# Windowed attention and a dense softplus block on one core: softmax two heads ahead instead of four, sink sums two steps later, exact loads without zeros, and new lists of the order

## The chip, the core and the metric

One core of a Trainium2 chip runs the kernel. The metric is device time in microseconds (us), the median of several executions. The trace comes from one profiled execution. Engines are named PE (TensorE), PEld (its weight loads), DVE (VectorE), ACT (ScalarE), POOL (GpSimd) and SP (SyncE, which issues nearly all DMAs).

## The reference

```python
# q, k, v: 4 x 8 heads x 768 x 64, float32; n_sink 4, window 128
scores = (q @ k.T) / 8
keep = (key < n_sink) | (0 <= query - key < window)
a = softmax(where(keep, scores, -1e9))
x = (a @ v), heads side by side          # 3072 x 512
h = x @ w_in                             # 512 x 2048, float64 weights
g = max(h, 0) + log1p(exp(-abs(h)))
out = g @ w_out                          # 2048 x 512, float64 weights
```

## The kernel before, in words

The 3072 rows are worked in 12 chunks of 256 (three to a batch of 768), each with 8 heads. A head of a chunk is one step of the attention, and one slice of 256 of the 2048 inner columns is one step of the dense part, whose slices run one chunk (8 steps) behind the attention. A loop over steps i calls the parts of several heads and slices, each at its own distance from i. Each part is a letter:

- L loads a head's keys and queries, p splits them into a rounded high part and a rest (ACT casts, DVE subtracts twice in `split_low`, called at h), S makes the scores on PE, T masks them and takes the row's largest (DVE), e exponentiates (ACT), N or M (two heads at once) inverts the sums (DVE), n scales (POOL or ACT).
- W transposes the weights on PE, t copies them out of PSUM (ACT or DVE), u takes the rest (DVE), B selects the window with four selects on POOL, V multiplies by the values on PE, O adds the halves up (ACT copy, two DVE adds).
- k and K make the four heads' weights on the sink keys: a product on DVE, a transpose on PE, ACT copies, and at y two DVE subtractions and a POOL copy. For an even head V also makes the sink part of a pair of heads with one matmul (line 422), which ACT copies to xs. Z adds it to the pair's sum, X rounds that to xh, x takes the rest xl.
- U is the up projection of a slice (24 matmuls of 256 columns, lines 564 to 582; H is its first half), F the three activations of the softplus (ACT), P the gate (DVE; it frees the PSUM bank of U, of which there are two), g rounds to gh, R takes the rest gl, D and E are the halves of the down projection (6 matmuls of 512 columns each), Y stores.
- G and q load and split values, J and j the sinks' values.

Chunks 0 and 1 are "exact": their heads aren't split, queries of two heads lie beside zeros in one tile (`q0`), so that each head's 64 rows meet keys of 128 partitions, and values likewise (`v0`, line 237), so that each head's matmul writes 128 partitions, half of them zeros.

The weights come in float64, 32 blocks of 512 KB, in the order in which the dense part wants them (wi00, wi01, wi10, wi11, wo00 and so on). Each goes through w (the DMA), a (the top words, line 502), c (the 32-bit word, DVE, line 516), d (the high part) and l (the low part). `WT`, `WH` and `WL` name the engine of a, d and l for each block (A, V for DVE, P for POOL), `WM` whether the word lies in SBUF (s) or PSUM (p; then l is DVE's); `NM`, `TH` and `GH` name those of n, t and g.

All engines run in order. Their orders are set by two lists written by hand or found by a search: `START` (lines 1021 to 1032) for the first 17 steps, where a token such as D1 calls one part at once and z11 issues 11 matmuls that only keep PE busy; then `STEADY` (lines 1011 to 1020), one string for each step modulo 8. A load waits for the buffer that it reuses: tiles "qk" (a split head, or queries of an exact pair) have two.

What sets the distances is this, in `_fast`:

```python
"S": (call(att, "scores"), G),          # G = 4: step i makes head i + 4
"p": (call(att, "split"), G + 1),
"W": (call(att, "weights_t"), c.LEAD),  # LEAD = 0
"k": (call(att, "sink_weights", G), 0),
"L": (call(att, "load"), G + 2),
```

Of the kernel before, what the change touches and what calls it, by code (L numbers as in the profile page):

```python
# [142 lines left out]
class _Attention:  # L143


    def __init__(self, c, chunk):
# [258 lines left out]
    def values(self, h):  # L405
# [19 lines left out]
        for n in range(self.vlo, 3):
# [5 lines left out]
            nc.tensor.matmul(x[:, :, o], w, pt[:, :, m], start=first, stop=last, skip_group_check=True)  # L431
        self.x[h] = x

    def out(self, h):
# [16 lines left out]
        if h % 2 == 1:  # L451
            xf, xs, hi, lo = self.xf, self.xsb, xh[:, h // 2], xl[:, h // 2]
            eng = "V" if h == H - 1 else c.E["xl"]

            def high():
                _copy(nc, c.E["xh"], hi, xf[:])
                c.do("x", lambda: _sub(nc, eng, lo, xf[:], hi))

            def total():
                (nc.vector if h == H - 1 else nc.gpsimd).tensor_tensor(xf[:], xf[:], xs[:], ALU.add)  # L460
                c.do("X", high)

            c.do("Z", total)

    def xs(self, h, t):
        c, nc, chunk = self.c, self.c.nc, self.chunk
        self.xsb = c.sp.tile([P, CT], F32, tag="xs", name=f"xs{chunk}_{h}s", bufs=1)
        _copy(nc, "A", self.xsb[:], t)
# [624 lines left out]
```

## Time and profile before

| | |
|---|---|
| median of 3 runs | 707.87 us (706.4 to 710.44) |
| profiled execution | 706.73 us, span 705.0 us, clock 0.998 |
| PE, PEld busy | 685.4 us (97%), 618.8 us (88%) |
| DVE, ACT, POOL busy | 578.5, 468.0, 377.3 us |
| HBM read, written | 57.40 MB, 6.29 MB |

The span runs from the first to the last instruction. Busy time of an engine counts its instructions' own time, and a row's idle time before them, with the instruction that ended it, tells what the engine waited for. A matmul's end is modelled, so successive matmuls overlap in the rows: the distance of their starts is their pace. PE's granted clock is full throughout the span.

### The profile page before, as it was taken

How to read it: one execution, taken by the hardware profiler on the slowest of the kernel's cores; microseconds unless marked ns; L12 is line 12 of the kernel's file. 1: busy time of each engine (PE TensorE's matmuls, PEld its weight loads, DVE VectorE, ACT ScalarE, POOL GpSimd, SP SyncE). 2: the span in 40 equal slices, each digit the busy share in tenths (PEclk: the TensorE clock that was granted, in tenths of full speed). 3: DMA queues.
4: the chain of work that ended last, by engine and by line, in shares of the span. 5: the costliest groups of instructions: out<-in, count | busy, mean ns of one | idle time of the engine just before them, and what ended most of it. 6: DMA issues, size and time to landing. Idle time of an engine off the chain costs nothing.

```text
span 705.0 us, 13763 instructions
## 1 busy us (share of the span) xinstructions
PE 685.4 (97%) x4454; PEld 618.8 (88%) x4454; DVE 578.5 (82%) x1679; ACT 468.0 (66%) x1176; POOL 377.3 (54%) x716
## 2 busy tenths in 40 slices
PE   7889899999999999999999999999999999999996
PEld 6778788899989999899999989999998989989995
DVE  6999888897898898897898898888898989865452
ACT  5889866667677666767676676767666676754331
POOL 5757465664465664664465565675555556452000
PEclk9999999999999999999999999999999999999999
DMA  8896623123122213221322321312212312100000
GB/s 312 290 384 225 198 73 103 51 73 95 47 81 81 68 52 87 78 66 54 95 69 62 99 70 54 111 47 66 85 51 77 95 46 80 62 13 1 31 2 34
DMA packets 39526, 64.67 MB, mean 92 GB/s; under 512 B 4502, under 2 KB 19990, under 8 KB 39446
## 3 DMA queue, kind: packets, MB, share of 16 engines
q1 hardware_dynamic: 39156, 63.19, 28.4%
q8 instruction: 37, 0.61, 0.4%
q10 hardware_dynamic: 290, 0.52, 0.2%
q14 instruction: 43, 0.35, 0.1%
HBM read 57.40 MB, written 6.29 MB: 90 GB/s over the span
## 4 chain that ended last, share of the span: by engine, by line
PE 85%; DMA 4%; DVE 4%; ACT 3%; POOL 1%; SPq 1%; issue 1%; POOLq 0%; DVEq 0%; ACTq 0%
PE h L575 36%; PE acc L637 12%; PE acc L639 12%; PE acc L638 12%; PE x L431 5%; PE s L278 3%; PE s L277 3%; PE t L371 2%; DMA wo21r<-w 1%; DMA wi71r<-w 1%; PE t L422 1%; DMA wi00r<-w 1%; DVE wt L516 1%; SPq L481 1%; ACT a L306 1%
## 5 line engine op out<-in xcount | busy, mean ns | idle before, releaser
L575 PE MATMUL h<-xh,wi 128*128 128x256 f32 x1536 | 251.9, 286 | 0.0
L575 PEld LDWEIGHTS h<-xh,wi 128*128 128x128 f32 x1536 | 211.4, 191 | 1.3 <-DVE mt L596 0.2
L637 PE MATMUL acc<-wo,gh 128*128 128x512 f32 x384 | 153.2, 399 | 2.2 <-ACT gh L57 2.2
L575 PE MATMUL h<-xl,wi 128*128 128x256 f32 x768 | 154.7, 283 | 0.0
L638 PE MATMUL acc<-wo,gh 128*128 128x512 f32 x384 | 150.8, 393 | 0.0
L639 PE MATMUL acc<-wo,gl 128*128 128x512 f32 x384 | 150.4, 392 | 0.3 <-DVE gl L65 0.3
L588 ACT ACTIVATE mt<-h 128x512 f32<-128x512 f32 x96 | 57.5, 599 | 125.9 <-PE h L575 125.6
L596 DVE SCALAR_TENSOR_TENSOR mt<-h,mt 128x512 f32<-128x512 f32 x96 | 66.0, 688 | 72.7 <-ACT mt L590 56.7
L575 PEld LDWEIGHTS h<-xl,wi 128*128 128x128 f32 x768 | 119.5, 192 | 0.1
L333 POOL TENSOR_SCALAR a<-a,rc 128x128 f32<-128x128 f32 x178 | 82.8, 477 | 34.8 <-DVE rc L319 33.8
L639 PEld LDWEIGHTS acc<-wo,gl 128*128 128x128 f32 x384 | 72.1, 188 | 17.0 <-DVE gl L65 0.7
L637 PEld LDWEIGHTS acc<-wo,gh 128*128 128x128 f32 x384 | 72.3, 188 | 14.7 <-ACT gh L57 2.6
L306 ACT ACTIVATE a<-a,stats 128x136 f32<-128x136 f32 x192 | 76.0, 397 | 13.1 <-DVE stats L297 12.9
L397 POOL TENSOR_SCALAR_AFFINE_SELECT pt<-th 128x256 fp32r<-128x256 f32 (+1 forms) x96 | 46.7, 486 | 66.2 <-ACT th L57 65.9
L638 PEld LDWEIGHTS acc<-wo,gh 128*128 128x128 f32 x384 | 72.4, 189 | 9.9
L397 POOL TENSOR_SCALAR_AFFINE_SELECT pt<-tl 128x256 fp32r<-128x256 f32 x80 | 43.8, 547 | 45.5 <-DVE tl L65 44.1
L65 DVE TENSOR_TENSOR gl<-mt,gh 128x512 fp32r<-128x512 f32 x96 | 67.6, 704 | 0.4 <-DVE gh L59 0.2
L589 ACT ACTIVATE mt<-mt 128x512 f32<-128x512 f32 x96 | 60.8, 634 | 3.1
L590 ACT ACTIVATE mt<-mt 128x512 f32<-128x512 f32 x96 | 60.7, 633 | 3.0
L57 ACT CAST qkh<-qk 128x656 fp32r<-128x656 f32 x80 | 59.0, 739 | 2.6 <-DVE wo L59 1.9
L65 POOL TENSOR_TENSOR vv<-vr,vv 128x384 fp32r<-128x384 f32 (+1 forms) x40 | 37.7, 942 | 29.1 <-ACT vv L57 28.6
L65 DVE TENSOR_TENSOR kl<-qk,qkh 128x400 fp32r<-128x400 f32 x80 | 50.9, 636 | 2.5
(198 smaller groups left out, 1249.8 us busy)
## 6 DMA issues: line engine op xcount, KB each, us to landing
qk<-qk SPq DMA_DIRECT2D x160, 164.0 KB, 2.9
out<-o SPq DMA_DIRECT2D x23, 256.0 KB, 2.1
vr<-v SPq DMA_DIRECT2D x28, 192.0 KB, 2.5
q<-q SPq DMA_DIRECT2D x7, 256.0 KB, 3.3
k<-k SPq DMA_DIRECT2D x8, 200.0 KB, 5.5
vz<-v SPq DMA_DIRECT2D x4, 384.0 KB, 8.2
vr<-v SPq DMA_DIRECT2D x12, 128.0 KB, 2.2
vz<-v SPq DMA_DIRECT2D x4, 256.0 KB, 5.8
```

The costliest lines, as they stand in the source:

```text
L57: nc.scalar.copy(out, in_)
L65: (nc.vector if eng == "V" else nc.gpsimd).tensor_tensor(out, a, b, ALU.subtract)
L306: nc.scalar.activation(a, a, AF.Exp, bias=c.stats[:, k : k + 1], scale=-1.0, accum_out=sm)
L333: (nc.vector if eng == "V" else nc.gpsimd).tensor_scalar(a, a, rc[:, j : j + 1], 0.0, ALU.mult, ALU.add)
L397: nc.gpsimd.affine_select(pt[:, e, :, 1], src[:], [[0, CH], [1, P]], ALU.is_ge, 0.0, base=0, channel_multiplier=-1)
L575: nc.tensor.matmul(h[:, j], wt, x, start=first, stop=last, skip_group_check=True)
L589: nc.scalar.activation(t[:], t[:], AF.Exp, scale=-1.0)
L590: nc.scalar.activation(t[:], t[:], AF.Ln, bias=1.0)
L596: nc.vector.scalar_tensor_tensor(t[:], h[:], 0.0, t[:], ALU.max, ALU.add)
L637: nc.tensor.matmul(acc[:], gh[:, j, q], wh, start=f == 0, stop=False, skip_group_check=True)
L638: nc.tensor.matmul(acc[:], gh[:, j, q], wl, start=False, stop=False, skip_group_check=True)
L639: nc.tensor.matmul(acc[:], gl[:, j, q], wh, start=False, stop=f == 2 * FP - 1, skip_group_check=True)
```

## The change

`AHEAD = 2` takes the place of `G` in the distances of S, T, N, M, p and L; k and K are called two steps later in the loop. The sink part of a pair leaves V and becomes a part of its own, C (`sink_sum`), called at steps 2 and 3 modulo 4. The first chunk's queries are loaded without zeros (each head's matmul then uses 64 rows of the array), the values of both exact chunks too (each head's matmul then has 64 columns). Engines of some steps, `START` and `STEADY` are new. Before, START made the scores of heads 0 to 20, now of 0 to 18.

```diff
+AHEAD = 2
@@ load
-                q = qp.tile([P, 2, CT], F32, tag=qt, name=f"q{chunk}_{h}", bufs=bufs)
-                (nc.scalar if chunk == h == 0 else nc.sync).dma_start(q[:], c.a["q0"][chunk, h // 2])
-                self.heads[h], self.heads[h + 1] = (q[:, 0], k), (q[:, 1], k)
+                if chunk == 0:
+                    q = qp.tile([P, CT], F32, tag=qt, name=f"q{chunk}_{h}", bufs=bufs)
+                    (nc.sync if h else nc.scalar).dma_start(q[:], c.a["q0"][h // 2])
+                    self.heads[h], self.heads[h + 1] = (q[:D], k[:D]), (q[D:], k[D:])
+                else:
+                    q = qp.tile([P, 2, CT], F32, tag=qt, name=f"q{chunk}_{h}", bufs=bufs)
+                    nc.sync.dma_start(q[:], c.a["q1"][h // 2])
+                    self.heads[h], self.heads[h + 1] = (q[:, 0], k), (q[:, 1], k)
@@ load_v
-            vz = pool.tile([P, 3 - lo, 2, P], F32, tag=tag, name=f"vz{chunk}_{g}", bufs=2)
+            vz = pool.tile([P, 3 - lo, 2, D], F32, tag=tag, name=f"vz{chunk}_{g}", bufs=2)
@@ values
-            if not odd:
-                sv = c.vs[self.b, h // G][:, h % G : h % G + 2].rearrange("p h d -> p (h d)")
-                t = _half_bank(c)
-                nc.tensor.matmul(t, sv, self.sk[h // G], start=True, stop=True)
-                self.xs(h, t)
-            nc.tensor.matmul(x[:, :, o], w, pt[:, :, m], start=first, stop=last, skip_group_check=True)
+            r = slice(h % 2 * D, h % 2 * D + D) if self.exact else slice(0, P)
+            nc.tensor.matmul(x[r, :, o], w, pt[:, :, m], start=first, stop=last, skip_group_check=True)
@@ out: the pair's total moves into sink_sum
+    def sink_sum(self, pair):
+        c, nc, chunk, g = self.c, self.c.nc, self.chunk, 2 * pair // G
+        sv = c.vs[self.b, g][:, 2 * pair % G : 2 * pair % G + 2].rearrange("p h d -> p (h d)")
+        t = _half_bank(c)
+        nc.tensor.matmul(t, sv, self.sk[g], start=True, stop=True)
+        xs = c.sp.tile([P, CT], F32, tag="xs", name=f"xs{chunk}_{pair}", bufs=1)
+        _copy(nc, "A", xs[:], t)
+        c.do("Z", lambda: self.total(pair, xs))
...
@@ _fast
+    def sums(i):
+        e = (i - AHEAD) % G
+        if e < 2:
+            call(att, "sink_sum", 2)(i - 2 + e)
-        "S": (call(att, "scores"), G),
+        "S": (call(att, "scores"), AHEAD),
-        "p": (call(att, "split"), G + 1),
+        "p": (call(att, "split"), AHEAD + 1),
-        "k": (call(att, "sink_weights", G), 0),
-        "K": (call(att, "sink", G), 0),
+        "k": (call(att, "sink_weights", G), AHEAD - G),
+        "K": (call(att, "sink", G), AHEAD - G),
+        "C": (sums, 0),
-        "L": (call(att, "load"), G + 2),
+        "L": (call(att, "load"), AHEAD + 2),
...
@@ engines
-Ctx.NM = "APPAAAPPPAPPAAPPP"
-Ctx.TH = "AAAAAAAAAAAVAAAAVA"
-Ctx.GH = "AAPAAAVVV"
-Ctx.WM = "spspsssppssspsssssssssssssssssss"
-Ctx.WT = "PAAVAVAAAAAPAAAVAVAAAAAAAAAPAAVP"
-Ctx.WH = "VPAAPVVAVAVAPAAAAAPAAAAAAAAAAAVV"
-Ctx.WL = "VPPVPVPPVPPVVPPPVVVPVPPVVVVVPVPV"
+Ctx.NM = "APPAAAPPPAPAAAPPP"
+Ctx.TH = "AAAAAAAAAAAVAAAVVA"
+Ctx.GH = "AAAAAPVVV"
+Ctx.WM = "spspsspppssppsssssssssssssssssss"
+Ctx.WT = "PAAVAVAAAAAPAAAVAVAAAAAAAAAVAAVV"
+Ctx.WH = "VPAAPVVAAAVAPAAAAAPAAAAAAAAAAAVV"
+Ctx.WL = "VVPVPVPPPVPVPPVPVVPPVPVVVVVVPVPV"
@@ STEADY
-    "kSWtpDuKYRQThqByUeFPXEngVZxON",
-    "SUpqWktYRZQDKuFTBXehEPNyngVxO",
-    "kpWYtuUByhqFQSDnTKePVZNROgXxE",
-    "WkZpSYUqQTtyhuFPRgDBEenXKVNOx",
-    "kpWYtUquKBSFRyZnQDVThePXNgOxE",
-    "kWUYtRuSTqDBQFepyZPEXNngVhKOx",
-    "knpWtuqUQKhYSTRDFeBZPVgyENOXx",
-    "kWpURYtSuDyqhBFTQPVOZeEgNXKnx",
+    "DWUptqSCQYyEFuhTkRePBNVgKXOZxn",
+    "QpSWYqUDtTFhEekuRNPBgVCyOnXZKx",
+    "pWYtQUkhKFySuqTPnDRxBeCEVXNZgO",
+    "YWQSqUtpDkuFhCTEePgBKNRxynVOXZy",
+    "WptQkUYuyKhXFqPnCSDTREBVxeNgZO",
+    "SWtquUDQEpFTeRkhYPBnyVgOZCNKxX",
+    "WpnUtkKhxyQSFuqDYCETPReBVNZOXg",
+    "YWSqUQtupBkFDChEVTyReOPNZKgXxn",
@@ START
-w J0 z1 S0 S1 T0 T1 w j4 w S2 S3 M0 w T2 S4 a w w T3 W1 c z3 a M2 S5 L8 T4 W0 z11 w S6 S7 T5 a w k0 d K0 c d
...
-l d U2 c F1 a T13 d V9 c D0 a L16 M12 c P1 d l l O8 l c R1 w W10 w O9 w a S14 w d D1 E0 d c U3 d l w a F2 c
-G12 d l l a a T14 L17 l W11 c P2 a c E1 N14 R2 V10 d c w l p16 S15 a F3 w O10 d G14 a d c L18 V11 d U4 P3
-T15 l l E2 l a c c w R3 a a d H5 W12 N15 D2 S16 k12 w O11 c D3 p17 d l F4 K12 a w U5 d G16 W13 l d a T16 l
-V12 P4 l w c L20 W14 S17 U6 c l F5 V13 a T17 E3 d P5 O12 c a U7 L19 R4 p18 E4 p20 J16 c S18 l l D4 F6 R5 l
-N16 D5 O13 p19 T18 W15 E5 S19 N17 G18 T19 L21 V14 q16 P6 F7 N18 c N19 S20 d V15 O14 d T20 L22 R6 W16 k16 O15
-U8 P7 K16 D6 R7 E6 F8 N20 V16 p21 O16 d P8
+w S0 z3 J0 S1 z3 S2 z3 T0 j4 T1 M0 T2 S3 w a z3 w w L8 T3 W1 S4 c a M2 S5 T4 w c k0 w W0 a S6 d z3 z3 S7 T5
...
+w a d H0 M10 k8 w V7 c c O7 d a S12 d l c U0 L16 F0 K8 U1 w a l a c w a d T12 P0 l L14 V8 c w d l d c a R0 w
+l W9 c S13 l a d F1 T13 d w U2 O8 a P1 c V9 D0 M12 a c d H3 l l R1 l c O9 W10 a S14 c d d l w a d F2 U3 l w
+a l c E0 D1 a w d l T14 G12 c P2 W11 c a w c V10 d l S15 p16 R2 a L17 F3 d w O10 c E1 d U4 P3 T15 d a l V11
+a w l G14 W12 D2 w R3 l S16 N14 w c N15 O11 c H5 D3 G16 a E2 c d L18 k12 p17 a F4 d K12 U5 l a w d W13 P4 d
+l V12 O12 c a T16 w W14 l a c E3 d F5 l S17 l T17 P5 R4 U6 a V13 c M16 U7 E4 p18 L20 O13 S18 L19 l c D4 l l
+J16 R5 V14 W15 F6 T18 P6 R6 O14 q16 D5 p19 E5 c V15 H8 O15 W16 F7 N18 U8 d G18 F8 P7 P8 D6 R7 d E6 d V16 O16
```

## Rows read from the trace of the kernel before

**Rows 1.** The page: busy time of PE over the span, and from the table of groups the largest one (busy us, mean ns of one, idle time before).

```profile
PE 685.4 (97%) x4454; PEld 618.8 (88%) x4454; DVE 578.5 (82%) x1679; ACT 468.0 (66%) x1176; POOL 377.3 (54%) x716
L575 PE MATMUL h<-xh,wi 128*128 128x256 f32 x1536 | 251.9, 286 | 0.0
```

**Rows 2.** Busy time by window, one steady chunk: window, its length, then busy us (instructions) of PE, PEld, DVE, ACT and POOL, PE's clock, the DMA engines' share and GB/s.

```profile
267.40:322.70 55.30, 55.30 (x368) 50.30 (x367) 47.91 (x140) 38.16 (x98) 33.43 (x64) 1.00 0.24 72
```

**Rows 3.** The same view, two windows of the start.

```profile
10.00:20.00 10.00, 7.88 (x49) 6.39 (x48) 8.31 (x39) 8.76 (x34) 4.51 (x10) 1.00 1.01 391
50.00:60.00 10.00, 7.54 (x45) 6.07 (x44) 9.54 (x21) 9.78 (x23) 6.46 (x6) 1.00 0.97 322
```

**Rows 4.** PE's waits from 0 to 110 us: who waited for whom, us in total, times, longest.

```profile
PE t L371 <- ACT sk L57: 4.1, 3, 2.4
...
PE s L277 <- DVE qkh L65: 1.2, 1, 1.2
```

**Rows 5.** The chain of work that ended last, from 57 to 112 us: start, us, what. Two of its pieces, an up projection and one matmul of a down projection.

```profile
107.60 2.87 PE h L575 x24
...
110.68 0.23 PE acc L637
```

**Rows 6.** DMA issues of the page: number, KB of one, us from issue to landing. The queries of exact chunks (an eighth is issued by ACT), and the values of chunk 1.

```profile
q<-q SPq DMA_DIRECT2D x7, 256.0 KB, 3.3
...
vz<-v SPq DMA_DIRECT2D x4, 384.0 KB, 8.2
```

**Rows 7.** POOL in order of time at the start: start, us, line, operation, output from input; in brackets the idle time before it and what ended it.

```profile
12.41 0.77 POOL L61 TENSOR_SCALAR upper<-wi00r 128x512 f16<-128x512 bf16 x1 [1.02 <-DMA wi00r<-w]
...
33.19 1.71 POOL L65 TENSOR_TENSOR wi<-wt,wi 128x512 fp32r<-128x512 f32 x1
...
73.43 0.79 POOL L61 TENSOR_SCALAR upper<-wi71r 128x512 f16<-128x512 bf16 x1 [4.01 <-DMA wi71r<-w]
```

**Rows 8.** DVE in order of time, same columns: the word of wi00, a word beside POOL's subtraction, gate P1, the end of the split of head 16, the split of head 21.

```profile
13.22 0.93 DVE L516 SCALAR_TENSOR_TENSOR wt<-wi00r,upper 128x512 int32<-128x512 int32 x1 [1.47 <-POOL upper L61]
...
33.69 1.77 DVE L516 SCALAR_TENSOR_TENSOR word_ps<-wi21r,upper 128x512 int32<-128x512 int32 x1
...
52.38 0.68 DVE L596 SCALAR_TENSOR_TENSOR mt<-h,mt 128x512 f32<-128x512 f32 x1
...
65.84 0.58 DVE L65 TENSOR_TENSOR kl<-qk,qkh 128x400 fp32r<-128x400 f32 x1
...
105.89 0.42 DVE L65 TENSOR_TENSOR qkh<-qk,qkh 64x256 fp32r<-64x256 f32 x1 [1.34 <-ACT qkh L57]
```

**Rows 9.** PE in order of time, same columns: scores S14; the first matmul of D1; transposes of sink weights (K12, 32 columns) and the up projection that follows; transposes W13; transposes W14 and the scores that follow.

```profile
50.55 1.06 PE L274 MATMUL s<-k,q 128*128 128x264 f32 x4
53.77 0.50 PE L637 MATMUL acc<-wo,gh 128*128 128x512 f32 x1 [2.17 <-ACT gh L57]
...
73.95 0.38 PE L352 MATMUL t<-ident,sa 128*32 128x128 f32 x2
74.08 0.72 PE L575 MATMUL h<-xh,wi 128*128 128x256 f32 x4
...
78.17 0.44 PE L371 MATMUL t<-ident,a 128*128 128x128 f32 x2 [2.41 <-ACT sk L57]
...
79.76 0.38 PE L371 MATMUL t<-ident,a 128*128 128x128 f32 x2
79.89 0.37 PE L277 MATMUL s<-qkh 128*128 128x264 f32 x1
```

**Rows 10.** ACT in order of time, same columns: the scalings of M12, gh of P1, the copy of the sink weights of K12.

```profile
51.92 1.28 ACT L331 ACTIVATE a<-a,rc 128x128 f32<-128x128 f32 x4 [0.15 <-DVE rc L319]
53.11 0.61 ACT L57 CAST gh<-mt 128x512 fp32r<-128x512 f32 x1
...
77.75 0.36 ACT L57 COPY sk<-t 32x256 f32<-32x256 f32 x1 [2.29 <-POOL sk L354]
```

**Rows 11.** SP's issues in order of time: the loads of heads 17 and 18.

```profile
64.08 1.20 SPq L214 DMA_DIRECT2D qk<-qk  x2
...
66.97 1.46 SPq L214 DMA_DIRECT2D qk<-qk  x2
```

**Rows 12.** All engines in order of time in a steady chunk, where K, S, D and the sink sum stand behind each other: K, POOL's copy at y, the last matmul of D, the sink sum.

```profile
295.63 0.27 PE L358 MATMUL t<-ident,sa 128*64 128x128 f32 x1
...
297.26 0.40 POOL L61 TENSOR_SCALAR sk<-sk 64x256 fp32r<-64x256 f32 x1 [0.82 <-ACT mt L588]
...
297.36 0.40 PE L639 MATMUL acc<-wo,gl 128*128 128x512 f32 x1
...
297.72 0.39 PE L422 MATMUL t<-sk,vs 128*128 128x256 f32 x1
```

**Rows 13.** The same view at the seam of two chunks: the values of head 7, and of the last pair xh, one step of the normalise and xl.

```profile
318.47 0.62 PE L431 MATMUL x<-pt,vv 128*128 128x256 f32 x3
...
320.89 0.41 ACT L57 CAST xh<-xf 128x256 fp32r<-128x256 f32 x1 [0.48 <-DVE xf L460]
321.11 0.16 DVE L318 TENSOR_SCALAR sm<-sm 128x2 f32<-128x2 f32 x1
321.31 0.17 DVE L319 RECIPROCAL rc<-sm 128x2 f32<-128x2 f32 x1
321.39 0.41 DVE L65 TENSOR_TENSOR xl<-xf,xh 128x256 fp32r<-128x256 f32 x1
```

More of the change, by code (lines that the diff above doesn't have):

```diff
@@ L151, in __init__ @@
         self.exact = chunk < c.EXACT
-        self.heads, self.v, self.a, self.rc, self.sk, self.pt, self.s, self.sm, self.x = {}, {}, {}, {}, {}, {}, {}, {}, {}
+        self.heads, self.v, self.a, self.rc, self.sk, self.pt, self.s, self.sm, self.x, self.xf = {}, {}, {}, {}, {}, {}, {}, {}, {}, {}
     def load_sinks(self):
@@ L445, in out @@
         if h % 2 == 0:
-            self.xf = c.sp.tile([P, CT], F32, tag="xf", name=f"xf{chunk}_{h}")
-        mine = self.xf[r0 : r0 + D]
+            self.xf[h // 2] = c.sp.tile([P, CT], F32, tag="xf", name=f"xf{chunk}_{h}")
+        mine = self.xf[h // 2][r0 : r0 + D]
         _copy(nc, "A", mine, x[D:, 0])
@@ L450, in out, with total, high @@
         nc.vector.tensor_tensor(mine, x[:D, 1], mine, ALU.add)
[L451 to L468, printed above, removed]
+    def sink_sum(self, pair):
[6 more added lines that the diff above has]
+        c.do("Z", lambda: self.total(pair, xs))
+    def total(self, pair, xs):
+        c, nc, xf = self.c, self.c.nc, self.xf.pop(pair)
+        xh, xl = c.x[self.chunk]
+        last = 2 * pair + 2 == H
+        (nc.vector if last else nc.gpsimd).tensor_tensor(xf[:], xf[:], xs[:], ALU.add)
+        def high():
+            _copy(nc, c.E["xh"], xh[:, pair], xf[:])
+            c.do("x", lambda: _sub(nc, "V" if last else c.E["xl"], xl[:, pair], xf[:], xh[:, pair]))
+        c.do("X", high)
 def _weight_dma(c, s, k, half):
@@ L746, in _fast @@
     parts = {
-        "S": (call(att, "scores"), G),
-        "T": (call(att, "softmax"), G),
-        "N": (call(att, "normalise"), G),
-        "M": (call(att, "normalise_two"), G),
-        "p": (call(att, "split"), G + 1),
+        "S": (call(att, "scores"), AHEAD),
+        "T": (call(att, "softmax"), AHEAD),
+        "N": (call(att, "normalise"), AHEAD),
+        "M": (call(att, "normalise_two"), AHEAD),
+        "p": (call(att, "split"), AHEAD + 1),
         "q": (call(att, "split_v", 2), 1),
         "W": (call(att, "weights_t"), c.LEAD),
-        "k": (call(att, "sink_weights", G), 0),
-        "K": (call(att, "sink", G), 0),
+        "k": (call(att, "sink_weights", G), AHEAD - G),
+        "K": (call(att, "sink", G), AHEAD - G),
+        "C": (sums, 0),
         "V": (call(att, "values"), 0),
@@ L1020 @@
 ]
 Ctx.START = """
-w J0 z1 S0 S1 T0 T1 w j4 w S2 S3 M0 w T2 S4 a w w T3 W1 c z3 a M2 S5 L8 T4 W0 z11 w S6 S7 T5 a w k0 d K0 c d
-N4 T6 l c G4 W2 a l L10 V0 V1 d O0 c l N6 G6 O1 W3 a w T7 d c V2 a O2 S8 a N5 N7 W4 V3 T8 L12 c S9 k4 O3 w w
-a z4 K4 c G8 G10 d T9 l W5 d w N9 S10 V4 l a W6 V5 T10 N8 d O4 O5 S11 W7 T11 w l c l z2 V6 V7 w O6 W8 w w a
-c M10 O7 c k8 d w l L14 a d d U0 F0 K8 w S12 l a U1 T12 V8 l c w a c d a P0 S13 c w l d w c d R0 a z2 l a W9
-l d U2 c F1 a T13 d V9 c D0 a L16 M12 c P1 d l l O8 l c R1 w W10 w O9 w a S14 w d D1 E0 d c U3 d l w a F2 c
@@ new lines @@
+K0 T6 d G4 w a W2 c c V0 l d V1 l l N6 O0 O1 a d W3 T7 c L10 w a a V2 z3 M4 S8 z3 w N7 G8 W4 L12 k4 V3 T8 c
+S9 c O2 O3 a G6 K4 w T9 d w G10 W5 d S10 a l l N9 W6 V4 T10 O4 w w N8 V5 d O5 w W7 l S11 T11 V6 W8 c w l O6
+w a d H0 M10 k8 w V7 c c O7 d a S12 d l c U0 L16 F0 K8 U1 w a l a c w a d T12 P0 l L14 V8 c w d l d c a R0 w
+l W9 c S13 l a d F1 T13 d w U2 O8 a P1 c V9 D0 M12 a c d H3 l l R1 l c O9 W10 a S14 c d d l w a d F2 U3 l w
+a l c E0 D1 a w d l T14 G12 c P2 W11 c a w c V10 d l S15 p16 R2 a L17 F3 d w O10 c E1 d U4 P3 T15 d a l V11
@@ L1061, in _layout @@
     k0 = np.ascontiguousarray(first[..., :KC]).reshape(Ctx.EXACT, H // 2, P, KC)
-    q0 = np.zeros((Ctx.EXACT, H // 2, 2, D, 2, CT), k.dtype)
+    q0 = np.ascontiguousarray(first[0, ..., KC:]).reshape(H // 2, P, CT)
+    q1 = np.zeros((H // 2, 2, D, 2, CT), k.dtype)
     for e in range(2):
-        q0[:, :, e, :, e] = first[:, :, e, :, KC:]
+        q1[:, e, :, e] = first[1, :, e, :, KC:]
     vb = v.transpose(0, 2, 1, 3).reshape(B, NB, P, H // 2, 2, D)
-    v0 = np.zeros((Ctx.EXACT, H // 2, P, 3, 2, 2, D), v.dtype)
+    v0 = np.zeros((Ctx.EXACT, H // 2, P, 3, 2, D), v.dtype)
     for n in range(Ctx.EXACT):
@@ L1069, in _layout @@
             i = n * CH - 1 + k
-            for e in range(2 * (i >= 0)):
-                v0[n, :, :, k, e, e] = vb[0, i, :, :, e].transpose(1, 0, 2)
+            if i >= 0:
+                v0[n, :, :, k] = vb[0, i].transpose(1, 0, 2, 3)
     return {
@@ L1074, in _layout @@
         "k0": k0,
-        "v0": v0.reshape(Ctx.EXACT, H // 2, P, 3, 2, P),
-        "q0": q0.reshape(Ctx.EXACT, H // 2, P, 2, CT),
+        "v0": v0,
+        "q0": q0,
+        "q1": q1.reshape(H // 2, P, 2, CT),
         "v": np.ascontiguousarray(v.transpose(0, 2, 1, 3)).reshape(B, NB, P, H * D),
```

## The prediction

> **What bounds the kernel now.** I read the busy table first: TensorE (PE) works 685.4 of 705.0 us, so all of its idle time is 19.6 us [rows 1] (a matmul counts there with its pipelined length). Then windows. A steady chunk of 55.3 us has PE busy for 55.30 [rows 2]: there the pace is PE's own sum of matmuls, and no reordering can win there, only lose. The idle time is at the start: 2.12 and 2.46 us in two 10 us windows, beside a VectorE (DVE) busy for 9.54 in the second [rows 3]. The table of PE's waits for that stretch names the releasers: transposes behind ScalarE's (ACT's) copy of sink weights (4.1 us in three), scores behind the split of a head (1.2) [rows 4]. So the reader looks for two things: which of these waits at the start go, and whether a steady step gets a new one. PE's own work is the same before and after (two heads' scores leave START and come back in the loop), so the sum is one of waits. One up projection is 24 matmuls in 2.87 us, one down matmul 0.23 [rows 5]; these measure distances below: 1.4 us for a D or E part (6 matmuls), 0.5 for a head's scores (4 of 0.12), about 0.2 for two transposes, 0.5 for values.
>
> **Loads without zeros.** Queries of the first chunk and values of both exact chunks halve: 256 KB to 128 for four q, 256 to 128 and 384 to 192 for four vz each [rows 6], 1.8 MB less in all. Of this, four q and two vz, 0.77 MB, are queued ahead of the first weight block, wi00. At the 391 GB/s of 10 to 20 us [rows 3] that is 2.0 us. GpSimd (POOL) waits for wi00 [rows 7], and DVE then for POOL, 1.47 us [rows 8]; the softmax work ahead of it on DVE is not earlier, so 1.47 is the most that comes through. Nothing if the issue of wi00, behind the same ten DMAs on SyncE (SP), sets it. I take -1.4, since DVE has no other wait there.
>
> **The first down projections.** D1 waits 2.17 us [rows 9] of the 2.46 in its window [rows 3]: its gh stands on ACT behind four scalings of M12, 1.28 us [rows 10], and gate P1 on DVE (52.38) behind c15, M12 and c16. The new START has P1 ahead of these, some 2 us earlier by two weight steps of 0.68 and a normalise, and puts H3, U3 and E0, over 4 us of PE work, ahead of D1. But H3 writes the PSUM bank that P1 frees and now stands right after D0, which S14 (from 50.55) and W10 (0.2) followed [rows 9]: PE reaches it near 50.35, P1 ends near 52.38 + 0.68 - 2 = 51.1, so H3 waits about 0.8 us. I take 2.46 less 0.8, -1.7; ends 0 and -2.46.
>
> **wi71 and POOL.** POOL waits 4.01 us for wi71 in order [rows 7]; selects, scalings and the memset of the sink weights are queued behind, ACT's copy waits 2.29 for that memset [rows 10], and a transpose on PE 2.41 for ACT [rows 9]. The new list gives this step to DVE, later. That frees POOL. But the loads are swapped (head 16 ahead of 14), so head 17's load now reuses head 16's buffer: SP is released not after the scores of head 15 (64.08) but after the split of head 16, which ends near 66.4 [rows 8], as head 18's load is now (66.97) [rows 11]. wi70 and wi71 stand behind it, 2.3 us later in the same clock, and DVE waits in order. Behind DVE's wait are gate P4 and split 17, and PE has U5, W13, V12 and E3 to cover them, about 5 us. I take half of 2.41, -1.2; ends -2.41 and +2.3.
>
> **Two heads fewer in START.** Before, p21 is the last split and scores 21 follow it at once; DVE waits 1.34 for ACT's cast [rows 8], PE 1.2 [rows 4]. With two heads ahead the last split (p19) has U8, D6, E6 and values before its scores. I take -1.2; ends 0 and -1.34. DVE is spared two softmaxes and two splits in START; no PE wait beyond these is credited to it.
>
> **Weights on other engines.** Three low parts and two upper words net go from POOL to DVE. DVE pays 0.68 a step, yet a POOL subtraction of 1.71 stretches the DVE step beside it to 1.77 [rows 7, 8], 1.1 more than 0.68. Three of each: +2.0 +0.7 against -3.3. On the path I take 0, ends -1 and +2.7. The changed letters of NM, TH, GH and WH and one more filler matmul lie in waits: 0, and 0.1 for the filler without them.
>
> **Narrow matmuls.** Values of 16 heads now use 64 columns of the array, scores of 8 heads 64 rows. In the trace transposes with 32 columns (73.95) let the next matmul start 0.13 later, and the full-width ones (79.76) also 0.13 [rows 9]: nothing for the width. I take 0; the other end is a rival. [...]
>
> **Sink sums two steps later.** Twice a chunk, K, S, D and then the sum C stand on PE: C comes 0.1 + 0.5 + 1.4 = 2.0 us after K. In one such place of the steady loop K starts at 295.63, POOL's copy ends at 297.66, and C starts at 297.72 instead of 297.59 [rows 12]: 0.13 lost. Before, one place a chunk has this distance, after, two: 10 chunks x 0.13 = +1.3; ends 0 and +8 (another POOL copy of 0.40 ahead at all 20). The softmax has two steps of nearly 7 us to reach W, more than its chain of DVE, ACT and POOL steps of under 1 us each: 0.
>
> **The seam of two chunks.** In the new order values of head 7 come after E, and U0 only after D and W: U0 starts 0.5 + 1.4 + 0.2 = 2.1 us after those values, and wants the last pair's xh after 18 matmuls, at 4.2, xl at 4.7. Today xh is there 2.83 and xl 3.33 us after the values begin [rows 13]; gate P (0.68, as at 52.38 [rows 8]) is put ahead of the total on DVE, for xh also the normalise (0.16 and 0.17): 3.85 and 4.0. ACT's exponentials stand ahead of its copy now. Slack 0.35 us; price 0, the other end is the first rival.
>
> **Sum.** -1.4 - 1.7 - 1.2 - 1.2 + 1.3 = -4.2 us. Against the profiled execution, 706.73 us (span 705.0 and 1.7 around it), that is 702.5; this execution is 1.1 below the median of 707.87, so on the median 703.7.
>
> **Rivals.** First, slower: the seam. From 0.35 us of delay on, every 0.1 late costs 1.0 us over ten chunks. Two DVE steps of that chain stretched as in [rows 8] add 2.2: (2.2 - 0.35) x 10 = +18.5, 722.2. For it: POOL has the preceding pair's xl and a scaling near that place. Against it: DVE's steps of the seam run beside POOL now too, and its normalise and subtraction took 0.16, 0.17 and 0.41 [rows 13]. Second, the array drains at each change of width: a matmul lasts 0.286 [rows 1] at a pitch of 0.12, so 0.17 is there to drain; 16 heads in and out, +5.3, 709.0. Against it: rows 9. Third, the waits only move: DVE was at 9.54 of 10 [rows 3], and the new order gives it the same weight steps by the same up projections; then the second and third terms are nought, and 703.7 + 2.9 gives 706.6. For it: the new wait of SP and H3's bank. Fourth, the new START also takes away short waits that I left standing, 2.12 us of idle time from 10 to 20 us [rows 3] and both rests of the second and third terms, 0.8 and 1.2: 4.1 more, 699.6.
>
> **Numbers.** A measurement of this kernel tells about 0.5%, 3.5 us, from no change. Forecast 0.50 (its own range 700 to 706.5: a third of it within 0.5%), fourth 0.14, third 0.18, second 0.08, first 0.10. Faster: 0.33 + 0.14 + 0.04 of the third = 0.51; slower: the first and 0.02 of the second, 0.12; the same 0.37. The range leaves out the first rival and the tail of the fourth: 697.5 to 709.5.
>
> **What would show it.** Right: no POOL wait for wi71; D1 without a wait on gh; the first steps of the loop without a wait for the split; a steady chunk still near 55.4. Wrong: a chunk of 56 or more with U's matmuls waiting for xl (first rival); values matmuls of the exact chunks starting later behind others than now (second); PE idle near 10 us before 105 us, under other names (third).

## The result and the profile after

The changed kernel takes 713.82 us (median of 7 runs, 712.46 to 718.69) against 709.0 for the kernel before beside it (7 runs, 706.4 to 712.0): the ratio is 1.0085, 95% interval 1.006 to 1.011. It is slower by 0.6 to 1.1%, where the forecast was 703.7 us and the range ended at 709.5. The profiled execution took 717.17 us with a span of 715.3, against 706.73 and 705.0 before: 10.3 us to explain, twice the 4.8 us between the medians, as the one lies 3.4 us above its kernel's median and the other 2.3 below. Where executions of a kernel lie over 1.5% above its fastest, the ratios below leave these out, one of six in e3 and four of six in e9, while the medians count all.

The page of the changed kernel, busy time of PE and the largest group, as [rows 1]:

```profile
PE 702.8 (98%) x4455; PEld 619.4 (87%) x4455; DVE 587.9 (82%) x1680; ACT 470.5 (66%) x1178; POOL 373.2 (52%) x709
L580 PE MATMUL h<-xh,wi 128*128 128x256 f32 x1536 | 252.3, 286 | 0.9 <-DVE mt L601 0.9
```

PE is *busier* than before, by 17.4 us, with one matmul more. That is the first thing to see: the loss isn't shown as idle time. The windows of the changed kernel, as [rows 2, 3] (the same columns), one of the start and one steady chunk:

```profile
10.00:20.00 10.00, 10.00 (x33) 6.53 (x33) 4.94 (x28) 5.80 (x23) 2.85 (x7) 1.00 0.99 365
270.11:326.46 56.35, 56.11 (x368) 50.27 (x368) 49.56 (x142) 38.54 (x97) 33.87 (x63) 1.00 0.24 71
```

From 10 to 20 us PE is busy for all of 10.00 us, yet with 33 instructions where it had 49 in 7.88 us [rows 3]: the busy share hides a slow array. And a steady chunk has the same 368 matmuls in 56.35 us instead of 55.30 [rows 2], with 0.24 us of visible idle time. So there are two losses, in two places.

PE in order of time at the start of the changed kernel (start, us, line, operation, shape, number; L280 are scores of the exact chunks, L755 the filler matmuls, L377 transposes of softmax weights):

```profile
1.88 3.78 PE L755 MATMUL word_ps<-sk 128*128 128x256 f32 x16 [1.88 <-POOL sk L70]
...
6.11 1.70 PE L280 MATMUL s<-k,q 64*128 64x136 f32 x4
7.74 1.01 PE L755 MATMUL word_ps<-sk 128*128 128x256 f32 x3
...
25.04 0.69 PE L377 MATMUL t<-ident,a 128*128 128x128 f32 x2 [0.51 <-ACT sk L58]
...
28.00 0.44 PE L377 MATMUL t<-ident,a 128*128 128x128 f32 x2
...
30.46 0.62 PE L755 MATMUL word_ps<-sk 128*128 128x256 f32 x3
```

The same three fillers take 1.01 us at 7.74 and 0.62 at 30.46, two transposes 0.69 at 25.04 and 0.44 at 28.00; the first sixteen fillers take 3.78 us, 0.24 each, where up matmuls of the same size have a pitch of 0.12 [rows 5]. So PE runs at about half pace until 28 us, though the column of the granted clock shows 1.00. That column takes from 1.00 only what the trace's entries of the clock take away, and the first entry of this trace lies at 27.97 us, where the full clock begins: the 1.00 ahead of it is no reading. In the kernel before the entries begin at 5.57 us and turn to half at 701.9, so its clock is known to be full between these two times and not throughout.

PE's waits from 0 to 110 us in the changed kernel, as [rows 4]:

```profile
PE word_ps L755 <- POOL sk L70: 1.9, 1, 1.9
PE t L377 <- ACT sk L58: 1.3, 3, 0.5
PE h L580 <- DVE mt L601: 0.9, 1, 0.9
PE x L422 <- DVE xl L66: 0.8, 2, 0.6
```

The waits that the forecast took away are gone: D1's on gh, the 2.41 us of W13 (0.24 at 80.59 now) and scores behind the last split. What stands behind each in the changed kernel, all engines in order of time, answering to [rows 7 to 9]:

```profile
12.44 0.72 POOL L339 TENSOR_SCALAR a<-a,rc 128x128 f32<-128x128 f32 x2 [4.14 <-DVE rc L325]
13.22 0.76 POOL L62 TENSOR_SCALAR upper<-wi00r 128x512 f16<-128x512 bf16 x1
16.19 0.69 DVE L521 SCALAR_TENSOR_TENSOR wt<-wi00r,upper 128x512 int32<-128x512 int32 x1
...
79.22 0.47 DVE L60 CAST upper<-wi71r 128x512 f16<-128x512 bf16 x1
80.59 0.44 PE L377 MATMUL t<-ident,a 128*128 128x128 f32 x2 [0.24 <-ACT sk L58]
```

POOL no longer waits for the load of wi00, but for the scalings ahead of it, which wait through DVE and ACT for the slow scores; DVE's word of wi00 is 3 us later than before, not earlier. wi71 is DVE's.

In the loop, all engines in order of time, where K, S, D and the sink sum C stand behind each other in step 2 of a chunk, as [rows 12] (L344 is the product of sink weights, L364 K, L458 C):

```profile
340.35 0.69 DVE L60 COPY o<-acc 128x512 f32<-128x512 f32 x1
341.07 0.23 DVE L344 TENSOR_TENSOR sa<-a,rc 128x64 f32<-128x64 f32 x1
341.45 0.27 PE L364 MATMUL t<-ident,sa 128*64 128x128 f32 x1 [0.15 <-DVE sa L344]
342.39 0.58 DVE L66 TENSOR_TENSOR sk<-t,sk 32x128 fp32r<-32x128 f32 x2
343.16 0.40 POOL L62 TENSOR_SCALAR sk<-sk 64x256 fp32r<-64x256 f32 x1 [3.13 <-DVE sk L66]
343.18 0.39 PE L644 MATMUL acc<-wo,gl 128*128 128x512 f32 x1
343.61 0.39 PE L458 MATMUL t<-sk,vs 128*128 128x256 f32 x1
```

K itself waits for a product that stands behind the copy of an output; C starts 0.43 us behind the last D matmul, where the pace is 0.23 and the kernel before had 0.36 [rows 12]. Over six steady chunks C's weight load waits for POOL's copy at 12 places, 5.4 us in all; the kernel before has 6 places and 2.3 us. And the seam, as [rows 13]: values of head 7, the first up projection, the last pair's xh and xl.

```profile
324.23 0.64 PE L433 MATMUL x<-pt,vv 128*128 128x256 f32 x3
...
326.22 0.72 PE L580 MATMUL h<-xh,wi 128*128 128x256 f32 x4
...
327.51 0.41 ACT L58 CAST xh<-xf 128x256 fp32r<-128x256 f32 x1 [2.24 <-DVE xf L467]
327.95 0.45 DVE L66 TENSOR_TENSOR xl<-xf,xh 128x256 fp32r<-128x256 f32 x1
...
328.82 0.31 PEld L580 LDWEIGHTS h<-xl,wi 128*128 128x128 f32 x2
```

xl ends at 328.40; the weight load that wants it starts at 328.82. The seam holds, with 0.42 us to spare.

### The profile page after: what moved, and what is told of

Read it like the earlier page. It is cut to its first block, busy times and chain, and to the rows that moved or that the text cites. A ratio compares the mean times of both kernels' runs of the same rounds, so it can differ in the third digit from the quotient of the medians.

```text
span 715.3 us, 13844 instructions
## 1 busy us (share of the span) xinstructions
PE 702.8 (98%) x4455; PEld 619.4 (87%) x4455; DVE 587.9 (82%) x1680; ACT 470.5 (66%) x1178; POOL 373.2 (52%) x709
## 4 chain that ended last, share of the span: by engine, by line
PE 82%; DVE 8%; ACT 6%; issue 1%; DMA 1%; POOL 0%; SPq 0%; POOLq 0%; ACTq 0%; DVEq 0%
PE h L580 33%; PE acc L642 10%; PE acc L643 10%; PE acc L644 10%; PE x L433 5%; PE t L377 3%; PE s L283 2%; PE s L284 2%; PE s L280 2%; PE t L458 1%; DMA wo70r<-w 1%; PE word_ps L755 1%; ACT upper L58 1%; ACT mt L594 1%; DVE mt L601 1%
## 5 line engine op out<-in xcount | busy, mean ns | idle before, releaser
L339 POOL TENSOR_SCALAR a<-a,rc 128x128 f32<-128x128 f32 x176 | 87.8, 510 | 108.6 <-DVE rc L325 108.6
L66 DVE TENSOR_TENSOR gl<-mt,gh 128x512 fp32r<-128x512 f32 x96 | 71.7, 747 | 0.4 <-DVE gh L60 0.2
L403 POOL TENSOR_SCALAR_AFFINE_SELECT pt<-th 128x256 fp32r<-128x256 f32 (+1 forms) x96 | 44.5, 463 | 46.2 <-ACT th L58 35.5
L58 ACT CAST qkh<-qk 128x656 fp32r<-128x656 f32 x80 | 59.3, 741 | 1.0 <-DMA qk<-qk 0.5
L66 POOL TENSOR_TENSOR vv<-vr,vv 128x384 fp32r<-128x384 f32 (+1 forms) x40 | 42.3, 1057 | 24.5 <-ACT vv L58 24.3
```

Source lines behind the costliest of these rows:

```text
L58: nc.scalar.copy(out, in_)
L66: (nc.vector if eng == "V" else nc.gpsimd).tensor_tensor(out, a, b, ALU.subtract)
L339: (nc.vector if eng == "V" else nc.gpsimd).tensor_scalar(a, a, rc[:, j : j + 1], 0.0, ALU.mult, ALU.add)
L403: nc.gpsimd.affine_select(pt[:, e, :, 1], src[:], [[0, CH], [1, P]], ALU.is_ge, 0.0, base=0, channel_multiplier=-1)
```

## The experiments

Theories. **A**: scores on 64 rows leave TensorE at half pace in the start. **B**: each change of width to the 64 columns costs. **C**, later **D**: in the loop, sink weights and selects on DVE and POOL come too late for PE. The rival to all: the new order of the start is late by itself. All results, with the start of chunk 3's first up projection (chunks counted from 0) and the length of the steady chunk 4 in the profiled execution:

| kernel | median us (runs) | ratio to before, 95% | chunk 3 starts | chunk 4 |
|---|---|---|---|---|
| before | 707.87 | | 211.71 | 55.30 |
| changed | 713.82 (712.46 to 718.69) | 1.0085 [1.006, 1.011] | 213.74 | 56.36 |
| e1_q_zeros | 709.46 (707.32 to 712.77) | 1.0017 [0.9994, 1.004] | 204.33 | 56.38 |
| e2_v_zeros | 716.81 (710.18 to 719.79) | 1.0104 [1.0067, 1.0141] | 207.19 | 56.37 |
| e3_steady | 712.2 (708.17 to 719.22) | 1.0039 [1.0009, 1.007] | 216.30 | 56.26 |
| e4_all_three | 705.87 (704.41 to 707.5) | 0.9965 [0.9946, 0.9984] | 205.34 | 56.20 |
| e5_chain | 703.57 (702.93 to 707.65) | 0.9941 [0.9916, 0.9966] | 202.71 | 55.74 |
| e6_chain_v_narrow | 704.42 (703.13 to 706.32) | 0.9943 [0.9926, 0.9961] | 204.56 | 55.74 |
| e7_q_onchip | 706.26 (704.14 to 708.39) | 0.9972 [0.9952, 0.9991] | 203.93 | 55.74 |
| b1_q_narrow | 711.22 (709.32 to 713.48) | 1.004 [1.0018, 1.0061] | 216.09 | 55.35 |
| e8_swap | 699.33 (698.62 to 701.46) | 0.9866 [0.9842, 0.989] | 202.73 | 55.34 |
| e9_loop_only | 708.97 (697.89 to 709.81) | 0.9896 [0.984, 0.9952] | 213.36 | 55.29 |
| e10_fillers | 700.85 (700.21 to 701.26) | 0.9877 [0.9856, 0.9898] | 204.40 | 55.30 |
| b2_v_narrow | 707.23 (706.0 to 709.26) | 0.9975 [0.9959, 0.9991] | 214.04 | 55.30 |

**Queries with zeros again (e1).**

```
-   q = qp.tile([P, CT], ...);  heads: (q[:D], k[:D]), (q[D:], k[D:])
+   q = qp.tile([P, 2, CT], ...);  heads: (q[:, 0], k), (q[:, 1], k)
```

> The changed kernel with the queries of the first chunk loaded with zeros again (scores of 8 heads use 128 rows of the array instead of 64). Theory A, the 64-row scores at the very start leave TensorE at half pace until about 31 us: the four fillers' and scores' pitches (0.34 and 0.44 us in the changed kernel up to 31 us) fall to about 0.12 to 0.2 from 6 us on, the first values matmul of head 0 starts near 19 instead of 26.5 us, and the time falls by 3 to 6 us, to about 709. Rival, the new order of the start is late for other reasons: the pitches may change, but chunk 3 begins no earlier than 213.98 us and the time stays within 1 us of 713.8.

PE of e1 in order of time:

```profile
6.70 0.71 PE L750 MATMUL word_ps<-sk 128*128 128x256 f32 x3
7.25 0.84 PE L275 MATMUL s<-k,q 128*128 128x136 f32 x4
7.72 0.71 PE L750 MATMUL word_ps<-sk 128*128 128x256 f32 x3
```

The three fillers take 0.71 us here instead of 1.01, the scores 0.84 instead of 1.70, from the same place in the same order. Chunk 3 starts 9.4 us earlier than in the changed kernel, 7.4 earlier than before. The median is 4.4 us less, as theory A had it, and the profiled execution 9.9 us less (707.32 against 717.17). The rival falls: the new order of the start isn't late by itself.

**Values with zeros again (e2), and the first mending of the loop (e3).**

```
-   vz [P, 3 - lo, 2, D];  x[r, :, o]  (r: the head's 64 rows of x)
+   vz [P, 3 - lo, 2, P];  x[:, :, o]
```

> The changed kernel with the values of the two exact chunks loaded with zeros again (values of 16 heads use 128 columns instead of 64). Theory B, a change of width costs about 0.09 us at each of 32 switches: the first matmul behind a values matmul, and the first values matmul behind another, start 0.09 us earlier, and the time falls by about 2.9 us, to 711. Rival, the switches are hidden or the longer loads (0.9 MB more) cost as much: within 1 us of 713.8, or later.

```
-   "pWYtQUkhKFySuqTPnDRxBeCEVXNZgO"   "WpnUtkKhxyQSFuqDYCETPReBVNZOXg"
+   "kpWYtQUhKFySuqTPnDRxBeECVXNZgO"   "WpnUtkKhxyQSFuqDYETPReBCVNZOXg"
```

> The changed kernel with two strings of the steady order mended: in step 2 the product of sink weights on VectorE goes ahead of the copy of the output (it is ready 0.7 us earlier, so the transpose of sink weights has no wait), and in steps 2 and 6 the sink sum goes behind the second down part (1.4 us later on TensorE). Theory C, the waits of these two cost 1.38 and about 1.6 us in six chunks, 0.5 us a chunk: a chunk goes from 55.81 to about 55.3 and the time falls by about 5 us, to 709. Rival, what waited there waits at the next place instead (values behind the selects, VectorE): the chunk stays above 55.7 and the time within 1.5 us of 713.8.

e2 can't tell anything of theory B: with narrow queries its executions lie 9.6 us apart. The profiled one, the fastest at 710.18 us, shows in order of time that the half pace isn't the same in every execution:

```profile
6.87 0.62 PE L754 MATMUL word_ps<-sk 128*128 128x256 f32 x3
...
16.67 1.70 PE L280 MATMUL s<-k,q 64*128 64x136 f32 x4
```

PE has the same instructions as in the changed kernel up to here. They went at full pace from about 6 us, then PE fell back to half from 16.1 to 22.9 us (granted clock 0.80 from 10 to 20 us, 0.86 from 20 to 30).

In e3 the chunk got 0.1 us shorter, not 0.5. Theory C falls as stated; its rival had the chunk right, and missed the time by 0.1 us (1.6 below 713.8 instead of 1.5).

**All three together (e4).** 

> The three edits together: queries and values with zeros again, and the mended strings. If theories A, B and C each hold and do not overlap, the gains add: 713.8 less 4.5, 2.9 and 5, about 701.5, faster than the kernel before by about 6 us, which is what two heads ahead and the new lists are worth by themselves. If the start's loss is made good later anyway, A and B overlap and it comes to 705 to 708. If the new lists lose by themselves, it stays above 709.

It is faster than before by 0.2 to 0.5%. The time lies where it was expected if A and B overlap, but for another reason: the chunk stays at 56.20. All engines in order of time in e4, in step 2 (L452 is C, L427 the values, L398 and L401 POOL's selects):

```profile
334.40 0.40 POOL L62 TENSOR_SCALAR sk<-sk 64x256 fp32r<-64x256 f32 x1 [3.01 <-DVE sk L66]
334.87 0.41 POOL L398 TENSOR_SCALAR_AFFINE_SELECT pt<-th 128x256 fp32r<-128x256 f32 x1
...
335.84 0.29 POOL L401 TENSOR_SCALAR_AFFINE_SELECT pt<-tl 128x128 fp32r<-128x128 f32 x1
335.84 0.28 PE L452 MATMUL t<-sk,vs 128*128 128x256 f32 x1
336.18 0.62 PE L427 MATMUL x<-pt,vv 128*128 128x512 f32 x2
```

C no longer waits, POOL's copy is done at 334.80. But the selects stand behind that copy, their last part ends at 336.13, and the values start at 336.18, 0.34 us behind C. POOL had idled for 3.01 us ahead of the copy, with th ready. That is theory D: not C's place, but the sink weights ahead of the selects.

**Selects ahead of the sink weights (e5), then scores ahead of the transposes (e8).**

```
-   "kpWYtQUhKFySuqTPnDRxBeECV..."    "WpnUtkKhxyQSFuqDYETPReBCV..."
+   "kpWYtQUhKuBFSyqTPnDRxeECV..."    "WpnUtkKhxuBQSyFqDYETPReCV..."
```

> Queries and values with zeros, as in e4, and in steps 2 and 6 of the loop the low part of the softmax weights and their selects on GpSimd put ahead of the sink weights' subtractions and of GpSimd's copy of them (the product of sink weights is ahead of the copy of the output and the sink sum behind the second down part, as in e4). Theory D, one chain is late in these two steps: the sink weights' copies stand on VectorE and GpSimd ahead of the 1.4 us of selects, so whichever matmul of TensorE comes first behind them (sink sum in the changed kernel, values in e4) waits; with the selects ahead neither waits, a chunk goes from 56.0 to about 55.4 and the time from 705.9 to about 700. Rival, the engines have no room for it in any order: the sink sum waits for GpSimd now, the chunk stays at 55.9 or more and the time within 1.5 us of 705.9.

The chunk is 0.46 us shorter, the time 2.3 us less, where theory D had 0.6 and about 6. The values now follow C at once, and the next wait shows, in order of time in e5 (L372 the transposes of the next head's weights, ACT's L58 the copy of the sink sum out of the bank):

```profile
332.52 0.28 PE L452 MATMUL t<-sk,vs 128*128 128x256 f32 x1
332.64 0.52 PE L427 MATMUL x<-pt,vv 128*128 128x512 f32 x2
332.97 0.35 ACT L58 COPY xs<-t 128x256 f32<-128x256 f32 x1
333.37 0.44 PE L372 MATMUL t<-ident,a 128*128 128x128 f32 x2 [0.21 <-ACT xs L58]
```

```
-   "YWQSqUtpDkuF..."   "YWSqUQtupBkF..."     (steps 3 and 7)
+   "YSWQqUtpDkuF..."   "YSWqUQtupBkF..."
```

> As e5, and in steps 3 and 7 the scores stand ahead of the transposes of the softmax weights. Theory D carried on: in e5 these transposes wait (0.19 to 0.23 us more at two places a chunk, and 0.06 within) for ScalarE's copy of the sink sum out of the bank; with 0.5 us of scores ahead they don't, a chunk goes from 55.75 to about 55.3 and the time from 703.6 to about 699.5, all of the loop's loss. Rival, something else takes its place again: the chunk stays at 55.7 and the time within 1 us of 703.6.

A steady chunk of e8, by window:

```profile
258.32:313.66 55.34, 55.34 (x368) 50.61 (x368) 48.09 (x142) 38.85 (x97) 33.68 (x63) 1.00 0.25 72
```

PE is busy for all of 55.34 us, as in [rows 2]; the loop's loss is gone, and e8 beats the kernel before by 1.1 to 1.6%.

**Values without zeros in e5 (e6) and in the kernel before (b2).** 

> As e5, but the values of the two exact chunks loaded without zeros, as in the changed kernel (64 columns of the array). Theory B, 32 switches of width at about 0.09 us: 2.9 us slower than e5, less up to 1 us for the shorter loads. Rival, no price: within 0.7 us of e5 or faster.

> The kernel before with the values of the two exact chunks loaded without zeros alone (64 columns of the array, 0.9 MB less to load). Theory B: the gaps behind these matmuls grow by 0.09 us, 2.9 us in 32 switches, of which the waits of the start hide some: 1 to 3 us slower than the kernel before. Rival, the shorter loads count for more: within 0.7 us or faster.

PE in order of time at one place, first in e5, then in e6:

```profile
45.86 0.40 PE L574 MATMUL h<-xl,wi 128*128 128x256 f32 x2
46.10 1.04 PE L427 MATMUL x<-pt,vz 128*128 128x128 f32 x6
46.90 0.48 PE L636 MATMUL acc<-wo,gh 128*128 128x512 f32 x1
```

```profile
47.03 0.40 PE L575 MATMUL h<-xl,wi 128*128 128x256 f32 x2
47.36 1.08 PE L428 MATMUL x<-pt,vz 128*64 128x128 f32 x6
48.37 0.50 PE L637 MATMUL acc<-wo,gh 128*128 128x512 f32 x1
```

From the two up matmuls to the first values matmul it is 0.33 us instead of 0.24: 0.09 at the change of width. From the first values matmul to what follows the six it is 1.01 instead of 0.80: 0.04 within and 0.17 on the way out. So the cost of theory B is there. At the other places of e6 it is likewise about 0.09 going in, 0.05 within and 0.09 or 0.17 going out; but at two of the 14 places two heads' narrow matmuls start 0.01 us apart, which saves 0.6 at each. Start to start, all 14 together cost PE 2.2 us. In the time that hardly shows: chunk 3 starts 1.85 us later than in e5, the medians lie 0.85 us apart, with intervals that overlap, and b2 is 0.1 to 0.4% *faster* than the kernel before. The whole price of narrow values, shorter loads included, these runs don't tell from nothing.

**Queries loaded without zeros, the zeros put in on the chip (e7).**

```
+   for e in range(2):
+       nc.vector.memset(q[D * (1 - e) : D * (2 - e), e], 0.0)
+       dma_start(q[D * e : D * e + D, e], q0[h // 2, D * e : D * e + D])
```

> As e5, but the queries of the first chunk are loaded without zeros and the zeros are put beside them on the chip by VectorE before, so the loads are those of the changed kernel and the scores use 128 rows. Theory A, the number of rows keeps TensorE at half pace: the fillers run at full pace from about 7 us as with zeros loaded, and the time is that of e5 or up to 1.5 us less. Rival, the shorter loads themselves or the order of arrival leave TensorE at half pace: fillers at 0.34 us until about 30 us and 7 us slower than e5.

With the short loads but 128 rows, three fillers take 0.71 us at 7.05: the loads have no part in the half pace. Nor does e7 gain: it is 2.7 us slower than e5. But it can't price the shorter loads: with eight loads instead of four and VectorE's zeros, wi00 is issued at 8.53 us instead of 6.13, and POOL's step on it, released by its load in both, starts at 13.57 instead of 12.53.

**Only the queries without zeros, in the old order (b1).** 

> The kernel before with the queries of the first chunk loaded without zeros alone (scores of 8 heads with 64 rows; order, values and all else as before). Theory A, 64 rows alone do it: fillers at half pace beyond 20 us, the first values matmul 5 us or more later than 18.35 us, and the time 2 to 7 us above the kernel before. Rival, it takes the new order of the start with its fillers in threes: TensorE at full pace from 6 us, and the time within 1.5 us of the kernel before or less.

b1 by window:

```profile
10.00:15.00 5.00, 4.82 (x15) 2.99 (x14) 3.16 (x20) 4.04 (x17) 2.71 (x7) 0.50 1.01 398
15.00:20.00 5.00, 5.00 (x25) 3.79 (x23) 2.30 (x11) 2.52 (x10) 1.06 (x4) 0.57 1.04 416
```

And PE of b1 in order of time:

```profile
6.24 0.95 PE L279 MATMUL s<-k,q 64*128 64x136 f32 x8
8.46 2.33 PE L279 MATMUL s<-k,q 64*128 64x136 f32 x8 [1.28 <-DVE stats L302]
...
12.95 0.99 PE L749 MATMUL word_ps<-sk 128*128 128x256 f32 x3
```

Here the granted clock itself says 0.50 from 10 to 15 us, and three fillers take 0.99 us: the pace that the changed kernel has up to 28 us. Eight narrow scores went at full pace at 6.24 (0.95 us); behind a wait of 1.28 us the next eight took 2.33. 64 rows alone make the kernel before 1 to 4 us slower. That is less than theory A had of it: the half pace ended at 19.3 us and not beyond 20, and PE's first matmul for the values came at 20.92, 2.6 us later than the 18.35 of before and not 5. The shorter query loads did bring something here: POOL's step on wi00 starts at 11.59 instead of 12.41 [rows 7] and DVE's word at 12.39 instead of 13.22 [rows 8].

**The loop alone mended (e9), then fillers (e10).** e9 is the changed kernel with the four strings of e8; e10 adds fillers to the start:

```
-   w S0 z3 J0 S1 z3 S2 z3 T0 j4 T1 M0 T2 S3 w a z3 w w      (e9)
+   w S0 z9 J0 S1 z9 S2 z9 T0 j4 T1 M0 T2 S3 w a z9 w w      (e10)
```

> The changed kernel with the loop of e8 alone: queries and values without zeros and the start as in the change. Theory D: the loop's loss goes (0.7 us in each of nearly ten chunks), about 707; chunk 3 still begins near 213 us where TensorE stays at half pace. Rival, the loop's waits only hide in the start's lateness: 712 or more.

> As e9, with nine filler matmuls instead of three at four of the first places between the scores of 64 rows. Theory A as a matter of the array's use: with many full-size matmuls between, TensorE reaches its full pace (fillers 0.12 us) before 16 us, and the time is 3 us or more below e9. Rival, fillers don't raise it: the 24 more of them take 0.34 each, the first values matmul comes 5 us or more later than in e9 and the time is 3 us or more above it.

PE of e10 in order of time:

```profile
5.85 0.94 PE L280 MATMUL s<-k,q 64*128 64x136 f32 x4
6.72 1.34 PE L755 MATMUL word_ps<-sk 128*128 128x256 f32 x9
7.99 0.94 PE L280 MATMUL s<-k,q 64*128 64x136 f32 x4
```

Nine fillers in 1.34 us, full pace from 7 us on, with the narrow scores unchanged between them. 24 matmuls more make the kernel 8.1 us faster than e9 by the medians (700.85 against 708.97), and chunk 3 starts 9.0 us earlier in the trace. e9's executions differ, though: 697.89, 706.57 and four from 708.89 to 709.81, the traced one among these; e10's five lie between 700.21 and 701.26. One execution of e9 was faster than all of e10, and the table's ratios, with only two executions of e9, don't tell the two kernels apart. So the 8.1 us are what most executions of e9 lost, not all.

The 64 rows as such are the smaller part of the loss: up to the next filler four of these scores take 0.87 us at full pace (5.85 to 6.72 in e10), 1.63 in the changed kernel (6.11 to 7.74), and 0.47 with 128 rows (7.25 to 7.72 in e1). The larger part is the clock: with these scores and few fillers it doesn't rise (the changed kernel until 28 us, e3 and e9 until 34) or falls back (e2 from 16.1 to 22.9 us, b1 from 9.1 to 19.3). These five traces have all 6.8 us or more at half pace between 9 and 40 us. Of the nine others eight have none there, and e4, with 128 rows, has it from 15.7 to 19.1. Why scores on 64 rows do this, and why it differs between executions, no run shows.

## Why the prediction was wrong, step by step

The 10.3 us of the two profiled spans come apart with e9 and e10, which have the change's start, loads and look-ahead. From before to e10 (loop mended, full clock) 705.0 to 698.4: -6.6. From e10 to e9 (half clock) 698.4 to 707.1: +8.7. From e9 to the changed kernel (its loop) 707.1 to 715.3: +8.2. These are single executions. The medians (707.87, 700.85, 708.97, 713.82) give -7.0, +8.1 and +4.9; the loop's 8.2 is borne out from the start of chunk 3 on, where the changed kernel's trace takes 7.9 us longer than e9's. That its median has less may come of the start: four of its seven executions, those from 712.46 to 713.82 us, have a mean granted clock of 0.988 to 0.991, near e2's traced one (0.993), the other three 0.998 or 0.999, as its own traced one. So most may have risen early and fallen back, as e2 did. That isn't traced.

- **The gain of the start: right in sum, in part by luck.** The four terms came to -5.5. With the clock out of the way (e10) chunk 3 starts 7.3 us earlier than before, of which 1.3 are the two heads that the last chunk gets back (its last stretch of up projections, from the first of chunk 10 to the first of chunk 11, grew from 53.16 to 54.44 us): 6.0. D1, W13 and the scores behind the split lost their waits as argued, priced at 4.1; H3's wait of 0.8 us didn't come, and a later up projection of the changed kernel waited 0.95 for a gate instead, a wait that e10 doesn't have. The term of the shorter loads, 1.4, isn't borne out there: POOL's step on wi00 waits for no load in e10, but DVE's word of it comes at 13.89, later than the 13.22 of before; in b1 it came 0.8 us earlier. What made the rest of the 6.0 no run tells.
- **Narrow matmuls at 0: the step that failed most.** I read rows 9, transposes with 32 columns, for what narrow matmuls cost behind them, and put the whole edit at nothing on the path, its scores with it. I also took PE's own work as the same before and after, so that the sum is one of waits; PE's busy time grew by 17.4 us. What I never asked is what the scores do to the clock at a place where the array is still at half pace (the first sixteen fillers take 0.24 us each) or has only just left it. It cost 8.7 us between the traces of e9 and e10 (8.1 by their medians, 4.4 between those of the changed kernel and e1), and no rival held it. For the values, a cost at each change of width is there in e6, as the second rival had it: 0.09 us going in, where the rival had 0.17, and 0.09 or 0.17 going out. The rival's 5.3 was my estimate, from the 0.286 of rows 1 and a pitch of 0.12; no run shows it: in e6 PE lost 2.2 us, and the medians hardly tell its price. That the array drains there isn't shown; the trace has only the later starts.
- **Sink sums at +1.3: mechanism near, size wrong by six.** The loop cost 8.2 us. I priced one wait, C behind POOL's copy. The trace has a chain: K behind a product that stands behind a copy of 0.69 us, the subtractions, POOL's copy, and behind that the selects. e3 and e4 took the first two waits away and gained 0.1 to 0.2 us a chunk, as values then waited for the selects; e5 moved the selects and the next transposes waited for the bank. Only with all of it mended (e8) was the chunk at 55.34. My upper end of +8 came near it, by another copy that isn't the cause, my value didn't: I took the wait of one place and didn't ask which instructions stand behind y on DVE and POOL.
- **The seam at 0: right,** with 0.42 us of slack instead of 0.35. A chunk of over 56 us came, which I had put down as the sign of the first rival, but without its wait for xl: a length alone doesn't name a cause.
- **Two heads ahead instead of four cost the loop nothing** by itself: e8 has it and runs chunks of 55.34. The order did.

## What to carry to other kernels

Where an engine's busy share is high, compare the number and the duration of its instructions with the other kernel's: at half pace 33 instructions filled 10.00 us here, where 49 took 7.88 before [rows 3]. When the rows of the first matmuls of a kernel are halved, check by the durations that the array still reaches its full pace there; 24 filler matmuls were worth 8 us here, between the medians of e9 and e10. And when a step is moved in a list that several engines share, write out what each of them now does between it and its user: a wait that is mended at one user moves to the next, until the engine that idles ahead of the chain (POOL, 3 us) gets the other work first.

## What the runs showed of the hardware

- Scores on 64 rows with fillers in threes left TensorE at half pace until 28 us in the changed kernel (three fillers 1.01 us at 7.74, 0.62 at 30.46); the same order with 128 rows (e1, three in 0.71 at 6.70), or with nine fillers (e10, nine in 1.34 at 6.72), ran at full pace from 7 us. It isn't so in every execution: e2 has the same scores and fillers and was at full pace from 6 to 16.1 us (three in 0.62 at 6.87). The first sixteen fillers of the changed kernel took 3.78 us, 0.24 each; its PE was then busy for all of the 10.00 us from 10 to 20 us and stayed at half pace.
- The granted clock read 1.00 through that stretch of the changed kernel, and 0.50 in b1 from 10 to 15 us, where the array had been at full pace before (eight scores in 0.95 us at 6.24), for the same pace of fillers (1.01 and 0.99 us for three). Ahead of the first entry of the clock (27.97 us in the changed kernel, 5.57 in the one before) the column reads 1.00, though the first sixteen fillers take 0.24 us each in both; so there durations tell the pace, not that column. From the first entry on, the two agree in the changed kernel: full clock at 27.97 us, two transposes in 0.44 us at 28.00.
- A change to 64 columns cost PE 0.09 us in e6 against e5, the way back 0.09 or 0.17; behind transposes of 32 columns the next matmul started 0.13 later, as behind full-width ones [rows 9].
